# Attention and a state-space convolution on one core: absolute phases taken by ScalarE, a smaller GpSimd descriptor area, more table buffers, sines of two groups next to each other, two products joined, a new order

## The chip, the cores and the metric

The kernel runs on one core of one Trainium2 chip. The metric is the device time of one execution in microseconds (us). Three runs of the kernel before gave 783.68, 779.48 and 782.46 us, so the median is 782.46 us.

The engines are named as the profile names them: PE is the matrix engine (PEld its weight loads), DVE the vector engine, ACT the scalar engine that evaluates functions from tables, POOL the GpSimd engine, and SP the engine whose queue issues nearly all transfers. The engines run their own lists of instructions in order, and wait for each other through semaphores. SBUF is the on-chip memory, PSUM the memory into which PE writes its sums.

## The reference

Two independent parts share the core, and their results stand beside each other in the output.

```python
def _A_ref(x, wqkv, wo):                      # B=1, S=2048, D=576
    H = 32; Dh = D // H; W = 256
    qkv = (x @ wqkv).reshape(B, S, 3, H, Dh).transpose(2, 0, 3, 1, 4)
    q, k, v = qkv[0], qkv[1], qkv[2]
    scores = jnp.einsum("bhqd,bhkd->bhqk", q, k) * (Dh ** -0.5)
    mask = (idx[:, None] - idx[None, :] >= 0) & (idx[:, None] - idx[None, :] < W)
    p = _softmax(jnp.where(mask, scores, -1e9))
    return concat_heads(p @ v) @ wo
def _B_ref(u, A_re, A_im, B_re, B_im, C_re, C_im, log_dt, Dskip):   # L=2048, N=128 states
    dt = jnp.exp(log_dt)[:, None]
    P = jnp.exp((dt * (A_re + 1j * A_im))[:, :, None] * l)
    K = jnp.einsum("dn,dnl,dn->dl", C_re + 1j * C_im, P, dt * (B_re + 1j * B_im)).real
    y = irfft(rfft(pad(u)) * rfft(pad(K)))[:L] + u * Dskip
```

Part A is attention in a window of 256 over 32 heads of 18. Part B builds, for each of 576 channels, a kernel `K` of 2048 taps from 128 complex exponentials, and convolves it with the input through a Fourier transform.

## The kernel before

**Stages.** `build` runs four lists of steps, one after the other: `front`, `tables`, `first` and `rest`. In each, several generators ("streams") hold the steps of one sort of work, and the strings in `PLAN` say which stream takes its next step. A letter lets a stream go on to its next `yield`; a letter with a digit runs a piece of work that a step left behind with `post` (an eviction from PSUM, a store). The engines' lists come out in just that order, so `PLAN` sets what stands behind what on every engine. The order isn't decided by a scheduler at build time; the conditions that the generators yield are not looked at there. `SLOTS` says which of three PSUM buffers (`ring0` to `ring2`, two banks each) each step of PE takes, and two more (`pp`) belong to the projection.

**front** loads the weights and the first input, finds the scales, splits the parameters of part B into three bf16 parts that GpSimd sends through DRAM (`prep`: the `nc.gpsimd.dma_start` calls; `prepw` loads the constants `c_ca`, `c_cp`, `c_ct`, `c_cm` the same way), and starts the projection to q, k and v.

**tables** holds the rest of the projection (`P`), the first transform of the input u (`U`, `s1_u`), and the taps of part B: 18 groups q of 32 channels, each in two halves c = 2q and 2q+1 of 16 channels. For a group:

- `t_factor` (PE, L505) writes logarithms and phases of 12 factors per channel into a ring buffer; ACT takes the exponentials (`mab`, L547), and `fold` brings the phase into one turn: ACT rounds it to an integer (L511), DVE subtracts that (L514), and DVE clears the sign bit of the result into a second half of the tile (L515), so that sine and cosine can both be had from the sine function. `t_phase` does the same for 32 phases per channel (tiles `fr`, one per half). `t_mg` makes the magnitudes, which ACT raises to exponentials inside the ring buffer (L527).
- `t_sin` is one block of six ACT instructions on both halves of `fr` and on `fa` (L556, L557, L561, L562). Exponentials and sines need different function tables, so loads (`ACT_TABLE_LOAD`) stand where the list goes from one to the other.
- `t_ab` and `t_prod` are POOL's: products of the factors (L567 to L577), then two products of 1024 elements for each half (L586) into `m0` and `m1`; there is one buffer for `m1`. `t_add` on DVE (L592) adds them.
- `t_q` on DVE multiplies cosines and sines with the magnitudes in four instructions of 512 elements (L601 to L604). `t_taps` on PE (L615) sums the taps, ACT evicts them (`Kq`, L621), and `t_dft` (L631, L635) transforms them; ACT and DVE each evict half of that (L647) and SP stores it.

The end of `tables` and all of `first` also hold the first steps of attention, among them `smax1` (letters `s`), which computes scores on PE (L906 to L917) for DVE's maxima (L940). **rest** holds the rest of attention (`scores`, `pv`, `norm`, `wo`) and of the convolution (`spectra`, `inverse`, `clast`).

The pools of the tables are `tab1` with one buffer of each tile (`fa`, `t1`, `t2`, `m1`), `tab2` with two (`mab`, `tr`, `A`, `Kq`, `kst`), and `frp` with `FR` = 3.

Of the kernel before, what the change touches and what calls it, by code (L numbers as in the profile page):

```python
# [42 lines left out]
def constants():  # L43
# [23 lines left out]
    for nm, v in mult.items():  # L67
# [19 lines left out]
        "AAAVCACAAAAAVAVVV1CV1CAVAVAAVCAV1ACCVCACCVVV1VV1CVCACBBPABV1CCPV1BV1CPCPP1PVP2PP4CPAPP1PP2BPCP1P4BVP"  # L87
        "CP",
    "tables":
        "GMGPGPG5G6G1PM1GG5GP2G2PGG6P4NMMG5P1G6G5G1P2PPNM1PP4G6P1GPG2UNRP2G1MMRXPP1M1P2P4X1RMGG5NG2PRMPGP1G5X"  # L90
        "X1M1XG6X5GP2RG6PMX2RNRUPGU2PMG1UP1PG5G2M1RGNU1XXX1UG6P2MPX1G5U2RG6PX4MU1XP4RRPM1X4PXPGX5X2P1GNMUMP2P"
        "1PX1PG1RXP2M1P4PG2X1GP4PG5MUNRU1PG5G6MX4U2G6XP1U4RPRM1PPPGX5P4P2P1NMRGPP2MNXXX4G5X2G1P1P4PM1X1G6G2P4"
        "P2U4X1XMGPMGX5G5RP1PG6M1PP2X2PP4NRPP4RPMP1MG1PP2PM1UX4PP1XGRX1NP4XG2PP2GX1MG5UX4G5MPG6U2G6X4P4RU1U4R"
        "P1M1X4XX2PPXMRNU4P2GPX5P1X1MNRP2PXG1G2P4PGM1X1PG5PPXP5X4GPPP5RX5UMG5G6PG6UPPNU1UX2MRRPP4U2M1U4UU2XPP"
        "5MMRX1PGP5P6UG1U1PM1PPPG2P5UX4NRU1PMPMGM1XPP5PX1U2RU4G5P5GG5PPG6RMGXG6PP5PRX2NP6NP4PPG1MG2XPPGX5PRM1"
# [1177 lines left out]
```

## Time and profile before

| | |
|---|---|
| median of three runs | 782.46 us (779.48 to 783.68) |
| the profiled execution's own time, from first to last instruction | 784.5 us |
| busy: PE, DVE, ACT, POOL | 693.0, 588.2, 534.3, 417.3 us |
| instructions | 29499 |

The page comes from one execution. "Busy" is the time in which an engine had at least one instruction running; PE's instructions are pipelined, so its busy time holds some waiting. A row of the list of groups names the line of the kernel, the engine, the operation, the tile written and those read with their sizes, how many there are, their busy time, the mean of one in ns, and the engine's idle time ahead of them with what ended it. A row of the waits names who waited, for whom, the total, how often, and the longest.

### The profile page before, as it was taken

What the parts mean: (1) busy time and instruction counts of PE and PEld (TensorE: products, weight loads), DVE (VectorE), ACT (ScalarE), POOL (GpSimd) and SP (SyncE); (2) the same over time, 40 slices, a digit from 0 to 9 for tenths busy, and PEclk for the clock granted to TensorE, in tenths of its full rate; (3) what the DMA queues carried; (4) which work ended last, traced back from release to release, by engine and by line L of the source; (5) the groups of instructions that cost most, each with busy time, mean ns of one, the idle gap of its engine ahead of it and who ended that gap; (6) DMA issues with size and microseconds to landing.
All of it is one profiled execution on the core that took longest, in us unless ns stands there. A gap on an engine that the chain in (4) does not pass through costs nothing.

```text
span 784.5 us, 29499 instructions
## 1 busy us (share of the span) xinstructions
PE 693.0 (88%) x12956; PEld 410.8 (52%) x12956; DVE 588.2 (75%) x779; ACT 534.3 (68%) x709; POOL 417.3 (53%) x309
## 2 busy tenths in 40 slices
PE   3786878998989989997789999989989998999997
PEld 2532444565545654665544555544555554557775
DVE  5998789998998897988777888876888586852100
ACT  2369577787887777773458677775877876786622
POOL 2245867987688666866007574451553444546120
PEclk9979799999999999996999999998999999899999
DMA  8998055738247537889578777676866786555786
GB/s 309 342 215 204 7 133 149 159 83 216 51 120 182 133 70 175 230 183 277 113 238 279 247 240 231 207 243 166 245 185 203 240 256 207 170 163 159 205 258 187
DMA packets 215904, 150.67 MB, mean 192 GB/s; under 512 B 103530, under 2 KB 195818, under 8 KB 215520
## 3 DMA queue, kind: packets, MB, share of 16 engines
q1 hardware_dynamic: 214160, 146.28, 66.0%
q0 software_dynamic: 1616, 2.52, 1.1%
q8 instruction: 101, 1.65, 0.8%
q14 instruction: 27, 0.22, 0.1%
HBM read 83.50 MB, written 65.11 MB: 189 GB/s over the span
## 4 chain that ended last, share of the span: by engine, by line
PE 55%; DVE 17%; ACT 15%; issue 6%; DMA 4%; SPq 1%; POOL 0%; ACTq 0%; DVEq 0%
PE po L1020 9%; PE pp L204 9%; PE ring L204 7%; PE ring L906 5%; DVE m L940 5%; PE ring L752 4%; PE ring L982 4%; PE ring L615 4%; PE ring L718 4%; PE ring L505 2%; DMA wraw<-in_wr_dram 2%; DVE amx L192 2%; PE ring L815 2%; ACT raw L1000 2%; DVE wl L372 2%
## 5 line engine op out<-in xcount | busy, mean ns | idle before, releaser
L940 DVE TENSOR_REDUCE m<-ring 128x2 f32<-128x640 f32 (+4 forms) x256 | 190.8, 779 | 66.0 <-PE ring L914 58.2
L586 POOL TENSOR_TENSOR m<-A,tr 128x1024 f32<-128x1024 f32 x72 | 141.5, 1983 | 52.6 <-DVE m L592 43.5
L1000 ACT ACTIVATE P<-ring,esc 128x1024 f32<-128x1024 f32 (+2 forms) x86 | 90.0, 1060 | 37.1 <-PE ring L995 32.7
L1000 ACT ACTIVATE raw<-ring,esc 128x1024 f32<-128x1024 f32 (+2 forms) x74 | 77.2, 1061 | 19.4 <-PE ring L995 18.8
L734 POOL TENSOR_TENSOR t<-X 128x768 f32<-128x768 f32 x24 | 46.7, 1944 | 76.1 <-ACT X L726 75.6
L1063 POOL TENSOR_TENSOR oh<-osb,oh 128x1024 f16<-128x1024 f32 x16 | 34.1, 2133 | 59.5 <-ACT oh L1059 42.9
L914 PE MATMUL ring<-sm,idb 64*64 64x128 bf16 x896 | 56.1, 224 | 3.3 <-issue 3.1
L204 PE MATMUL pp<-xh,wh 128*128 128x512 f16 x180 | 48.1, 397 | 10.0 <-DVE qst L453 5.0
L204 PEld LDWEIGHTS <-wh 128*128 128x128 f16 x324 | 30.7, 99 | 49.1 <-issue 11.7
L615 PE MATMUL ring<-Q,m 128*32 128x64 f32 x2304 | 42.9, 231 | 12.8 <-ACT fa L511 4.1
L1055 POOL TENSOR_TENSOR osb<-osb,T 128x1024 f32<-128x1024 f32 x16 | 38.6, 2410 | 25.8 <-DVE T L1050 23.8
L592 DVE TENSOR_TENSOR m<-m,m 128x1024 f32<-128x1024 f32 x36 | 51.6, 1432 | 0.7 <-POOL m L586 0.6
L615 PEld LDWEIGHTS ring<-Q,m 128*32 128x32 f32 x2304 | 36.9, 117 | 27.2 <-ACT mab L547 5.5
L906 PEld LDWEIGHTS <-raw 54*64 54x64 f16 x704 | 28.6, 108 | 41.1 <-issue 37.7
L740 POOL TENSOR_TENSOR Y<-t,t 128x384 f32<-128x384 f32 x24 | 24.7, 1029 | 46.1 <-DVE t L734 33.8
L906 PE MATMUL ring<-K,raw 54*64 54x320 f16 (+4 forms) x576 | 44.8, 308 | 4.5 <-ACT raw L1000 0.8
L204 PE MATMUL pp<-xh,wl 128*128 128x512 f16 x180 | 48.0, 400 | 0.6 <-DVE wl L372 0.6
L567 POOL TENSOR_TENSOR tr<-tr,mab 128x768 f32<-128x768 f32 x18 | 33.3, 1850 | 28.4 <-ACT tr L562 28.4
L726 ACT ACTIVATE X<-ring 128x768 f32<-128x768 f32 x48 | 36.7, 812 | 14.3 <-PE ring L718 8.1
L995 PE MATMUL ring<-tm,idb 64*64 64x256 bf16 (+2 forms) x640 | 45.0, 257 | 0.0
L982 PEld LDWEIGHTS <-K 55*64 55x64 f16 x1280 | 28.8, 108 | 26.7 <-issue 22.7
L752 PE MATMUL ring<-Y,i 32*64 32x192 f32 x768 | 38.7, 336 | 3.3 <-issue 2.3
(171 smaller groups left out, 1725.1 us busy)
## 6 DMA issues: line engine op xcount, KB each, us to landing
gk<-kst SPq DMA_DIRECT2D x36, 256.0 KB
gx<-ust SPq DMA_DIRECT2D x16, 576.0 KB
xk<-gx SPq DMA_DIRECT2D x24, 384.0 KB
xk<-gk SPq DMA_DIRECT2D x24, 384.0 KB
h<-ho SPq DMA_DIRECT2D x48, 192.0 KB
hp<-h SPq DMA_DIRECT2D x24, 384.0 KB
K<-kz SPq DMA_DIRECT2D x14, 512.0 KB
raw<-qz SPq DMA_DIRECT2D x11, 512.0 KB
```

What stands on the lines that cost most here:

```text
L204: self.nc.tensor.matmul(ps, u, v, start=(i == 0), stop=(i == len(ops) - 1))
L586: tt(m[part], A[:, ch, a0:a0 + 8].unsqueeze(3).to_broadcast(sh), tr[:, ch, part, 0:8].unsqueeze(2).to_broadcast(sh), op=OP.mult)
L592: self.nc.vector.tensor_tensor(m[0], m[0], m[1], op=OP.add)
L615: nc.tensor.matmul(kp[32 * st:32 * st + 32, j, :], m[:, ch, 32 * term:32 * term + 32], Q[:, ch, term, :], start=(term == 0), stop=(term == ...
L734: mul(ts[i], X[:, :, :, :192].rearrange("p i s j -> p s i j"), X[:, i, :, 192:].unsqueeze(2).to_broadcast(sh), op=OP.mult)
L752: nc.tensor.matmul(ps[64 * (b % 2):64 * (b % 2) + 64, b // 2, 192 * s:192 * s + 192], self.i1[32 * b:32 * b + 32, t, o:o + 64], Y[32 * b:3 ...
L906: nc.tensor.matmul(ps[z:z + 64, b, :n], d["Q"][rr, 2 * b + pp, 64 * qb:64 * qb + 64], d["K"][rr, 2 * b + pp, k0:k1], start=True, stop=Fals ...
L914: nc.tensor.matmul(out, self.idb[rr], self.sm[rr], start=False, stop=True, skip_group_check=True)
L940: self.nc.vector.tensor_reduce(out, x, axis=AX.X, op=OP.max)
L982: nc.tensor.matmul(ps[z:z + 64, b, off:off + w], d["K"][rr, 2 * b + pp, kc:kc + 64], d["Q"][rr, 2 * b + pp, q0:q0 + w], start=(k == 0), st ...
L1000: nc.scalar.activation(P[:, :, lo:hi], ps[:, :, lo:hi], AF.Exp, scale=self.esc)
L1020: nc.tensor.matmul(po[32 * p:32 * p + 32, z, q0:q0 + w], V[64 * z:64 * z + 64, kb * 76 + 19 * p:kb * 76 + 19 * p + 32], P[p % 2][64 * z:64 ...
```

## The change

Six edits are made at once.

1. `fold` no longer clears the sign bit on DVE. `t_sin` has ACT do it, with the function `Abs`, just ahead of the sine that reads the result: two of 128x512 and one of 128x384 in each group.
2. In `t_q` the products of cosine and sine with the upper half of the magnitudes become one instruction of 1024 elements, which reads the two halves of the tile in exchanged order.
3. The descriptor area that GpSimd's transfers use in SBUF is set to 2048 bytes per partition.
4. `FR` goes from 3 to 5; `fa` gets a pool of its own with two buffers (`fap`), and `tr` one with three (`trp`).
5. All four strings of `PLAN`, and `SLOTS`, are new.
6. As part of the new order, `t_sin` of two groups stands next to each other in some places, with no load of a table between them.

```diff
 PLAN = {
     "front":
-        "AAAVCACAAAAAVAVVV1CV1CAVAVAAVCAV1ACCVCACCVVV1VV1CVCACBBPABV1CCPV1BV1CPCPP1PVP2PP4CPAPP1PP2BPCP1P4BVP"
+        "AAACVAAAVCAAAVAAV1V1VCACVVV1AAAAVCAV1VCVV1CVCCCCAPV1CVCBBCBVACAV1V1VVCPCBPPPP1CP2P4PPPP1CP2P4PBCBPP1"
...
             nc.vector.tensor_tensor(k, x, k.bitcast(I32), op=OP.subtract)
-            nc.vector.tensor_scalar(f[:, 1].bitcast(I32), k.bitcast(I32), 0x7FFFFFFF, None, op0=OP.bitwise_and)
             self.n[end] += 1
...
-            f = self.fa[q] = self.p["tab1"].tile([128, 2, GC * 12], F32, name="fa")
+            f = self.fa[q] = self.p["fap"].tile([128, 2, GC * 12], F32, name="fa")
...
         for c in (2 * q, 2 * q + 1):
             f = self.fr[c]
+            nc.scalar.activation(f[:, 1], f[:, 0], AF.Abs)
             nc.scalar.activation(f[:, 0], f[:, 0], AF.Sin, scale=-TWO_PI)
             nc.scalar.activation(f[:, 1], f[:, 1], AF.Sin, scale=-TWO_PI, bias=self.halfpi)
         f = self.fa.pop(q)
-        tr = self.tr[q] = self.p["tab2"].tile([128, GC, 2, 12], F32, name="tr")
+        tr = self.tr[q] = self.p["trp"].tile([128, GC, 2, 12], F32, name="tr")
         v = lambda z: z.rearrange("p (c m) -> p c m", m=12)
+        nc.scalar.activation(f[:, 1], f[:, 0], AF.Abs)
...
-        tt(Q[:, :, 0, 32:64], cs, m[:, :, 32:64], op=OP.mult)
+        tt(Q[:, :, :, 32:64], f.rearrange("p i (c m) -> p c i m", m=32)[:, :, ::-1],
+           m[:, :, 32:64].unsqueeze(2).to_broadcast([128, HC, 2, 32]), op=OP.mult)
         tt(Q[:, :, 0, 0:32], cs[:, :, ::-1], m[:, :, 0:32], op=OP.mult)
-        tt(Q[:, :, 1, 32:64], sn, m[:, :, 32:64], op=OP.mult)
...
-            self.FR = 3
-            for n, b in (("tab1", 1), ("tab2", 2), ("frp", self.FR), ("P0", 2), ("Qp", 2)):
+            self.FR = 5
+            for n, b in (("tab1", 1), ("tab2", 2), ("frp", self.FR), ("P0", 2), ("Qp", 2), ("fap", 2), ("trp", 3)):
...
-    nc = _bacc.Bacc("TRN2", target_bir_lowering=False, num_devices=1)
+    nc = _bacc.Bacc("TRN2", target_bir_lowering=False, num_devices=1, dynamic_dma_scratch_size=2048)
```

How the new order stands on the engines is seen at two places. The first is ACT's list, where it takes the sines of a group. Before, each group's block has a load ahead of it and one behind it (buffer numbers are left out; `tr` holds the sines of the factors, `halfpi` is the constant that makes a cosine):

```order
L450 ACTIVATE qst<-pp 128x512
L556 ACT_TABLE_LOAD
L556 ACTIVATE fr<-fr 128x512
L557 ACTIVATE fr<-fr,halfpi 128x512
L556 ACTIVATE fr<-fr 128x512
L557 ACTIVATE fr<-fr,halfpi 128x512
L561 ACTIVATE tr<-fa 128x32x12
L562 ACTIVATE tr<-fa,halfpi 128x32x12
L511 ACTIVATE fr<-ring 128x512
L547 ACT_TABLE_LOAD
```

In the changed kernel, at one such place, the sines of a group are followed by three evictions and the two shown first here, and then by the sines of the next group, with the rows of L556 and L562 as the new `Abs`; the load for the exponentials comes only behind them:

```order
L623 ACTIVATE Kq_1281<-ring_1248 128x256
L623 ACTIVATE Kq_1281<-ring_1284 128x256
L556 ACTIVATE fr_1156<-fr_1156 128x512
L557 ACTIVATE fr_1156<-fr_1156 128x512
L558 ACTIVATE fr_1156<-fr_1156,halfpi_153 128x512
L556 ACTIVATE fr_1194<-fr_1194 128x512
L557 ACTIVATE fr_1194<-fr_1194 128x512
L558 ACTIVATE fr_1194<-fr_1194,halfpi_153 128x512
L562 ACTIVATE fa_1154<-fa_1154 128x384
L563 ACTIVATE tr_1364<-fa_1154 128x32x12
L564 ACTIVATE tr_1364<-fa_1154,halfpi_153 128x32x12
L547 ACT_TABLE_LOAD
```

The block of a group is nine rows instead of six. Over the whole list there were 37 loads of a table and there are 27: 18 groups had 18 loads ahead of their sines and have 13, so five pairs of groups share one, and the loads that go back to the exponentials (at L527 and L547) fall from 18 to 13; one stands at the start in both.

The second place is DVE's list near the start of `tables`, with the folds (`fr`, `fa`), the low halves of q and k (`qst`), and the products `Q`. Before:

```order
L514 TENSOR_TENSOR fr_516<-ring_485,fr_516 128x512
L515 TENSOR_SCALAR fr_516<-fr_516 128x512
L514 TENSOR_TENSOR fa_520<-ring_470,fa_520 128x384
L515 TENSOR_SCALAR fa_520<-fa_520 128x384
L453 SCALAR_TENSOR_TENSOR qst_556<-pp_450,qst_556 128x512
L601 TENSOR_TENSOR Q_588<-fr_474,ring_507 128x16x32
L602 TENSOR_TENSOR Q_588<-fr_474,ring_507 128x16x32
L603 TENSOR_TENSOR Q_588<-fr_474,ring_507 128x16x32
L604 SCALAR_TENSOR_TENSOR Q_588<-fr_474,ring_507 128x16x32
L592 TENSOR_TENSOR m0_579<-m0_579,m1_580 128x1024
```

And now, where L515 is the subtraction and L594 the sum of POOL's products:

```order
L515 TENSOR_TENSOR fr_593<-ring_571,fr_593 128x512
L515 TENSOR_TENSOR fr_595<-ring_591,fr_595 128x512
L515 TENSOR_TENSOR fa_634<-ring_562,fa_634 128x384
L515 TENSOR_TENSOR fa_639<-ring_617,fa_639 128x384
L454 SCALAR_TENSOR_TENSOR qst_621<-pp_499,qst_621 128x512
L594 TENSOR_TENSOR m0_602<-m0_602,m1_603 128x1024
L454 SCALAR_TENSOR_TENSOR qst_678<-pp_573,qst_678 128x512
L603 TENSOR_TENSOR Q_698<-fr_518,ring_680 128x32x32
L605 TENSOR_TENSOR Q_698<-fr_518,ring_680 128x16x32
L606 SCALAR_TENSOR_TENSOR Q_698<-fr_518,ring_680 128x16x32
```

The 54 rows that cleared sign bits are gone, four rows of products have become three, and the folds of the factors of two groups (`fa_634`, `fa_639`) follow each other, which one buffer for `fa` didn't allow. In the tables POOL's list has the same rows in the same order as before, and the same 12 transfers ahead of them; SP issues the same number of transfers. PE has the same matmuls: up to the last taps its list holds the same ones but for 16 more at L906, 12 more at L914, 4 more at L917, 12 fewer at L982 and 4 fewer at L995.

More of the change, by code (lines that the diff above doesn't have):

```diff
@@ L86 @@
     "front":
[L87 to L88 removed]
+        "AAACVAAAVCAAAVAAV1V1VCACVVV1AAAAVCAV1VCVV1CVCCCCAPV1CVCBBCBVACAV1V1VVCPCBPPPP1CP2P4PPPP1CP2P4PBCBPP1"
+        "PP",
     "tables":
[L90 to L91 removed]
@@ new lines @@
+        "PMNRU4X1P4GP2NXX2PG1PPP1G2X5P2RRMM1UUU2U1PGG5XPX1MMPM1GG6RXX1MG5P4P4G6PP1P1P2NGG1G2P2P4P4XX5PX2MGG5G"
+        "G5G6G6PPU4M1UUPPRRRMUNNX4RXX1X4X4U1PU2U4P1P1XP2UU1U2U4PUX1P2UNU2RU1PPPPP1P2P4XGX2G1X4PP5PRX5P4P4MM1P"
+        "G2PP5GGX4X4RMPG5PPP5PG6G5G6MM1XX1MMM1RPGNPPPP5G1G2PMMP5M1XX1PRPRPPXX2NRP5RMPGG5PPPP5G6X5X4PXXPX1X1GG"
+        "5G6XPP5PPPNRNP1P2MM1PPX4PX5X2X4X4GGPRRMP1P2G1G5XG6X1GRG2MG5M1G6PP1MU4GP4NG1G2GG5G6PPMP2M1MMM1XP4PPX1"
+        "UUMNU1PUU2XX5RRP1X2PP2XX1P1P4UP4RU4U2U1U4GP2G5NG6NPURPPP1MP2PPM1P4UU2U1PXU4RRX1P1MMPPM1XMX5PRX2MM1XP"
@@ new lines @@
+        "2GG1PPX4X1MNG2GP1PG5P2P4GG6G5P6P6GG1PPRG2P1GG6RPG5G6RMP5M1XX1XX4P4P2X2PPPPPNXMPGX5G5RRP6XG6P6X4P5PPP"
+        "5X1X1NRNXPX4X2P5PP4ZPPP5UGGG5G6G1PPPP5RRMG2M1MX4X4PPX5PPPUUU2PPU1UU1U2P5XU4P6RMX1M1MMM1MPP5PPP1PXX4X"
+        "4GPG5G6GX1NRG1G2XX2X5PP1P2P6MP2GGG5ZZG6RPM1PMRPG5G6U4XPNPRUP4P1UU1U2P4P2PP1P4UUPP4U2X1U1ZP2UMM1MMM1X"
+        "X1MNNPPPPRXRXP1X2P2X1X5GPRRGPG1G2X4X4G5G6P4MM1P6MPXX1X4PP6P1P1XX2X5P2NMP2M1GGG1G2PPPPG5G6MUUPRNRU4U2"
+        "U1UU4U1P4X4GP1U2P4P2U4G5G6PGP1MG5G6PM1ZXX1PPP5P2RRMMXM1MPPPX1PPss2sss2s2ss2sss2s2PP5P4sss2X4Ps2sss2s"
@@ new lines @@
+        "s4vassa1vs2s2ss2LaLsvvva1saa1s2s2Lss2vvv1ss2sas2c3c2aa1Lvssls6a1ass2s2c6n3aa1a1vss2aksa1aa1s2vkkscs2"
+        "c1asc3c6s4a1vvsss2s2ds2Lc2sd1s2ava1kcc1naasc3vd4s2va1a1saa1s2vsc2s2sads2a1ssld1kvsn1s2c6c3s2kkcLLLs2"
+        "c1ss6aa1sdss2n6sv1n4d4Lvvd4d1s2s2sss2s2ass2vala1saa1la1vvss2ss2s2vkss2ass2n3vc6s4aa1a1c2sdn1d1d4fs2c"
+        "3ss2aa1n6ssvs2Laa1svvv1s2Ls2sLss6s2ss2ss2cc1ss2aaa1a1svs2saa1aa1s2fee1asvnva1ss2as2ss2vaa1a1ssvvs2s2"
+        "d4Lss4an3s2n4n1ss2vnaa1a1aa1kn6asa1fs2kvfvvv1aa1see1s2asc2a1vLLs2asn3s6a1dd1c6c3ncc1aa1llLLsss2s2van"
@@ new lines @@
+        "4a1sn1ss2s2vss2sks2vss2n4aa1svsvls2s2skks2ss2dc2c6c3d1s4ss2cc1llaa1d4ss2dlsvs2Lss2d1d4aa1sLLvaa1e4s2"
+        "saa1s6c6ss2n3vvaa1ss2sss2s2aan6v1c2a1vsva1sas2s2asa1a1kvvn1kss2ks2n6aa1svvs2ss2sss2ss2vcc1c3s2fvs4ss"
+        "dlLLs2d1ys2c2c6c3scc1s2sLs6aaa1da1c2afa1Lsvd4d4d1n4nn3s2vv1c6ee1asLva1ss2aa1s2ss2vsn1sn6ke4s2s2ava1s"
+        "as2ss2n4sa1ss2s2asa1ss2s2vlaaskvs2va1a1ss4c3as2a1ss2aa1kncLc1vaa1sdd1s2ss6aa1LLssn3s2s2n1kkvssss2s2s"
+        "2vvayasv1vvn6s2ss2a1a1aa1sn4vssls2s2ssvs2d4s2s2ava1ac2aa1ss4Lva1ss2as2a1ss2vasLc6Lava1a1s2sas6ca1c1L"
@@ new lines @@
+        "sc3aa1vnn3ks2ass2a1dvd1d4d4c2v1ss2saa1svs2Ls2sas2a1ss2vn1lssss2s2s2avaa1sss2vs2vs4a1aa1fssvfan6s2ss2"
+        "s2Laa1La1Lnvee1sc6cvfc1s2ss6sc3s2aa1svvv1fs2c2e4sc6s2c3faa1s4fesksve1s2ss2s2svas2ss2vaa1a1ss2ss2aa1s"
+        "vss2s2ass2vaa1sss2s2vss2a1aa1kckc1kaLLLa1ss6n3nvaaa1a1lc2ddd1Lsss2vn4n1ve4s2ksd1n6ss2s2ss2vv1sc6cc1l"
+        "ls2svs2asss2s2vsa1aa1c3c2ee1svs2c6sc3kks2s2scc1s2vaa1ss2ss2kvvlasc6lls4wa1ww1s2ss6aa1aa1ddd4d4d1n4d1"
+        "cd4n4vvc2c1aaa1a1wc3wn3n1kc2kdnw1n3vvd1n1aaa1a1wkaa1akffc6c3n6v1wwww4a1w4w1Lcw1c1e4e4c6van6a1aaa1vfc"
@@ L143 @@
+    "2120102102102102101201021012012012021020120210210210201021021102102102102012101210210212012012012012"
+    "0210210120120120120120120121021020102102110210201201201202101201201210210120120120120121201201201201"
+    "201202012012012012120121021"
 )
```

63 lines of the change are left out of this document (19 added, 44 removed).

## The prediction

> **What bounds the kernel now.** I read the page for the shares of the engines, then split the span at 62 us (first load for sines) and at 384 us (last rows of `t_dft`).
>
> ```profile
> 62.00:384.00 322.00, 282.87 (x4027) 168.58 (x4025) 280.35 (x388) 239.20 (x381) 233.90 (x183) 0.95 0.60 145
> 384.00:784.50 400.50, 371.00 (x8797) 221.01 (x8789) 256.70 (x335) 269.16 (x295) 166.09 (x104) 0.98 0.71 215
> PE 55%; DVE 17%; ACT 15%; issue 6%; DMA 4%; SPq 1%; POOL 0%; ACTq 0%; DVEq 0%
> ```
>
> The columns of the windows are the stretch, its length, and the busy time of PE, PEld, DVE, ACT and POOL, then PE's granted clock, the share of the transfer engines and GB/s. Up to the last taps PE is busy 282.9 of 322 us and DVE 280.4; PE idles 39.1 us. Behind it PE is busy 371.0 of 400.5 us and no other engine is near that. In the chain (third row) PE has 55%, DVE 17%, ACT 15%. So the second stretch is PE's, and what the edits to the tables can win lies in the first one: PE's 39.1 us of idle time, and no more. Its waits there, by releaser:
>
> ```profile
> PE pp L204 <- DVE qst L453: 5.3, 5, 2.2
> PE ring L615 <- ACT fa L511: 4.1, 1, 4.1
> PE ring L615 <- DVE fa L514: 2.5, 3, 1.4
> PE ring L505 <- ACT ust L498: 2.3, 4, 1.0
> ...
> PE ring L631 <- ACT ust L498: 0.2, 1, 0.2
> ```
>
> These are the first four and the last of 30 rows. The 16 that name DVE sum to 22.1 us, the 13 that name ACT to 15.6, one transfer has 0.4. None is long: PE is held up a little everywhere, because an eviction or a factor comes late from an engine whose list is nearly full. POOL is held by DVE too, since its second product needs the one buffer of `m1` back:
>
> ```profile
> POOL m L586 <- DVE m L592: 43.5, 17, 5.1
> POOL tr L567 <- ACT tr L562: 28.4, 14, 7.9
> ```
>
> **DVE gives up 54 us.**
>
> ```profile
> L592 DVE TENSOR_TENSOR m<-m,m 128x1024 f32<-128x1024 f32 x36 | 51.6, 1432 | 0.7 <-POOL m L586 0.6
> L515 DVE TENSOR_SCALAR fr<-fr 128x512 int32<-128x512 int32 x36 | 35.7, 992 | 1.2
> L514 DVE TENSOR_TENSOR fr<-ring,fr 128x512 f32<-128x512 f32 x36 | 24.6, 682 | 5.2 <-ACT fr L511 4.9
> L601 DVE TENSOR_TENSOR Q<-fr,ring 128x512 f32<-128x512 f32 x36 | 24.5, 680 | 7.6 <-ACT ring L527 4.9 <-PE ring L615 2.0 <-ACT fr L557 0.7
> L603 DVE TENSOR_TENSOR Q<-fr,ring 128x512 f32<-128x512 f32 x36 | 24.4, 679 | 0.0
> L515 DVE TENSOR_SCALAR fa<-fa 128x384 int32<-128x384 int32 x18 | 13.2, 733 | 0.6
> L514 DVE TENSOR_TENSOR fa<-ring,fa 128x384 f32<-128x384 f32 x18 | 9.9, 551 | 8.1 <-ACT fa L511 8.0
> 60.24 0.43 DVE L515 TENSOR_SCALAR fr<-fr 128x512 int32<-128x512 int32 x1
> 61.77 0.36 DVE L515 TENSOR_SCALAR fa<-fa 128x384 int32<-128x384 int32 x1
> ```
>
> Both groups of L515 go: 35.7 + 13.2 = 48.9 us, of which 48.1 lie in the stretch (the last two rows run ahead of it, 0.43 and 0.36 us). The joined product of 1024 elements isn't in the trace. It can't be shorter than one of its halves (0.68), and the longest mean for 1024 elements is L592's 1.432 against 2 x 0.68 = 1.36 for the pair, so the 36 of them save between 24.4 us and nothing, or cost 2.6. L514's two sizes give 0.682 - 0.551 = 0.131 us for 128 elements, so 1.21 us for 1024; I take that: 36 x 0.15 = 5.4 us saved. DVE's list falls from 280.4 to 280.4 - 48.1 - 5.4 = 226.9 us.
>
> **ACT takes on 19 us.**
>
> ```profile
> L556 ACT ACT_TABLE_LOAD x18 | 23.1, 1283 | 0.3
> L556 ACT ACTIVATE fr<-fr 128x512 f32<-128x512 f32 x36 | 22.4, 623 | 0.4 <-DVE fr L515 0.2
> L511 ACT ACTIVATE fr<-ring 128x512 int32<-128x512 f32 x36 | 21.5, 598 | 11.9 <-PE ring L505 9.4 <-POOL wi L338 1.7 <-DVE Q L604 0.6
> L547 ACT ACT_TABLE_LOAD x14 | 18.0, 1283 | 5.1 <-PE ring L505 4.9
> L561 ACT ACTIVATE tr<-fa 128x384 f32<-128x384 f32 x18 | 9.1, 507 | 0.0
> 67.00 0.60 ACT L511 ACTIVATE fr<-ring 128x512 int32<-128x512 f32 x1
> 67.61 1.28 ACT L547 ACT_TABLE_LOAD   x1
> 68.91 0.49 ACT L547 ACTIVATE mab<-ring 128x384 f32<-128x384 f32 x1
> ```
>
> An `Abs` has no row; a sine without a bias tile of the same sizes has 0.623 and 0.507 us, a copy 0.598. By the sines 36 x 0.623 + 18 x 0.507 = 31.5 us come on (by the copy 1 us less). Ten loads of 1.283 us go, 12.8 us. Net +18.7: ACT's list in the stretch grows from 239.2 to 257.9 us of 322. The last three rows show what a change of tables costs: the instruction ahead ends at 67.60, the load runs from 67.61 to 68.89, the next starts at 68.91, so hardly anything beside the 1.28 us.
>
> The Trainium skill, ScalarE: Activation LUTs, section "What ACT_TABLE_LOAD costs", adds a drain of 1.38 us to each load, 2.66 us together; by that ten loads would give back 26.6 us and ACT would grow by only 4.9. The trace shows no such drain between these three rows.
>
> **The rest of the edits.** The small descriptor area touches GpSimd's 12 transfers at the start.
>
> ```profile
> q0 software_dynamic: 1616, 2.52, 1.1%
> 37.16 0.56 POOL L252 DMA_DIRECT2D c_ca<-in_c_ca_dram  x1
> 40.28 0.51 POOL L308 DMA_DIRECT2D Tim<-splim  x1 [0.43 <-issue]
> Tre<-splre POOLq DMA_DIRECT2D x1, 432.0 KB, 6.4
> Tim<-splim POOLq DMA_DIRECT2D x1, 432.0 KB, 7.0
> c_cm<-in_c_cm_dram POOLq DMA_DIRECT2D x1, 384.0 KB, 5.0
> 56.43 0.33 PE L505 MATMUL ring<-c_ca,Tre 96*128 96x384 bf16 x1
> ```
>
> Six of them are issued within 3.1 us and the last one lands at 40.3 + 0.5 + 7.0 = 47.8 us; PE reads it first at 56.4. If nothing has to wait for room, the cost is nothing. At worst each waits until the one ahead has landed: 4 x 5.0 + 6.4 us put the last issue at 63.6 and its landing near 70.6 us, 14 us after PE asks for it. I take nothing, since the whole queue moves only 1616 packets in the span, and keep the 14 us for the range. The added buffers cost no instruction; what they hide is in the sum below. The new order of `first` and `rest` rearranges the same work in a stretch where PE idles 400.5 - 371.0 = 29.5 us. I take zero and keep 4 us either way, a seventh of that idle time, which is a choice and not a measurement.
>
> **The sum.** It can be made in two ways. At most all 22.1 us that PE waits for DVE go, with nothing in return. Or the four engines stay as well filled together as before: 282.9 + 280.4 + 239.2 + 233.9 = 1036.4 us in 322 us is a sum of shares of 3.22; with 282.9 + 226.9 + 257.9 + 233.9 = 1001.6 us the stretch would last 311.2 us, 10.8 less. The first leaves out that ACT, which takes over from DVE as the fullest helper (257.9 against 226.9 us), will release PE later at places. The second leaves out that POOL, behind DVE for 43.5 us, will get `m1` back sooner, and that five `fr`, two `fa` and three `tr` let PE and ACT run further ahead. I take 15 us between the two. What is late next is PE itself, 282.9 us of then 307, with ACT behind it. The front isn't shortened. So the profiled execution would last 784.5 - 15 = 769.5 us; the median of the runs is 2.0 us below that execution's own time (782.46 against 784.5), which gives **767.5 us**.
>
> **Rivals.** *ACT takes it back.* The `Abs` stands between the fold and the sine in ACT's list, where DVE did it beside ACT, so a group's block there lasts nine instructions, 1.75 us longer, and evictions from `ring` and `pp` stand behind it. PE already waits 15.6 us for ACT; if those waits double, as the waits for DVE shrink by about as much, nothing is left: 780 to 784 us. Against it, ACT idles 82.8 us in the stretch and mostly because PE has nothing for it:
>
> ```profile
> ACT Kq L621 <- PE ring L615: 29.8, 18, 9.8
> ACT kst L647 <- PE ring L635: 10.4, 8, 2.9
> ```
>
> *Slower, by the same place.* If PE stands at ACT's blocks in nearly every group, with its three `ring` buffers full, the whole 18.7 us lengthens the stretch while DVE's relief opens nothing: 782.5 + 18.7 = 801 us, or 792 with half of it. It decides from the point at which each of the 18 groups loses over 1 us more to ACT than it gains from DVE (22.1 / 18 = 1.2 us at most). For it speaks the one wait of 4.1 us for `fa` from ACT; against it that the other 12 rows of ACT reach 2.3 us at most in total each.
>
> The Trainium skill, ScalarE: Activation LUTs, section "Rules for kernel authors", speaks for this rival: simple operations belong on VectorE, which it calls up to about three times faster per element, in bf16. In this trace, in fp32, the 128x512 took 0.992 us on DVE and the sine of that size 0.623 on ACT, so the trace does not agree.
>
> *The small area stalls GpSimd*: the tables start up to 14 us late, and with the gain the time is about 781. It is the case in which the change doesn't do what it says, as the room for more buffers isn't free. *More than forecast*: if the free time on DVE and the added buffers let PE be filled to 96% in the stretch, more than the 93% behind it (371.0 of 400.5), it lasts 282.9 / 0.96 = 295 us, 27 less: 755 us. For it speaks that no wait of PE there is longer than 4.1 us; against it that PE has never been that full over such a length.
>
> **How the numbers follow.** A measurement of this kernel can tell about 0.5%, 4 us, from no change: below 778.5 is faster, above 786.4 slower. The forecast, with a gain of 8 to 23 us, has 0.60; more than that 0.11; ACT or the small area taking it back 0.18; slower 0.11. Forecast alone: 759 to 775. The range reaches up to the rivals without a gain and down to the one with more: 753 to 783. Faster 0.71, same 0.18, slower 0.11.
>
> **What would show it.** DVE's busy time should fall from 588 to about 534 us, with no row that clears sign bits and a joined product near 1.2 us; ACT's should rise from 534 to about 553, with 27 loads of 1.28 us. The last taps should end near 367 us instead of 382, PE's waits for DVE ahead of that should halve and its waits for ACT grow by some 5 us; POOL's 43.5 us for the sum on DVE should shrink. Behind the last taps the span should still be about 400 us. The prediction is wrong if the last taps come no earlier (then it is ACT, and PE's waits name it), if PE's first L505 comes later than 56 us (then it is the area), or if the second stretch differs by over 4 us.

## The result and the profile after

The changed kernel takes 788.91 us (median of 20 runs, 782.15 to 795.07) where the kernel before, measured beside it, takes 782.48: a ratio of 1.0081, with an interval of 1.0054 to 1.0108. It is slower by some 6 us, where 15 us less were forecast. The profiled execution took 794.09 us with a span of 792.3, so it is one of the slower ones, 5 us above the median.

The page of the changed kernel, with the engines' busy time and the chain that ended last:

```profile
PE 693.5 (88%) x12956; PEld 405.8 (51%) x12956; DVE 544.7 (69%) x689; ACT 547.8 (69%) x753; POOL 413.9 (52%) x309
PE 46%; DVE 17%; ACT 15%; DMA 11%; issue 6%; SPq 4%; POOL 2%; ACTq 0%; DVEq 0%; POOLq 0%
```

DVE has 43 us less than before (588.2) and ACT 13.5 more (534.3). In the chain 11% are transfers now (4% before) and 4% SP's queue (1%). The windows, cut at the first load for sines and at the last rows of `t_dft` (columns as in the prediction), first the kernel before in its tables, then the changed one in all three stretches:

```profile
61.30:384.00 322.70, 283.55 (x4028) 168.83 (x4027) 281.02 (x389) 239.90 (x381) 233.90 (x183) 0.95 0.60 145
```

```profile
0.00:69.70 69.70, 40.43 (x145) 22.16 (x146) 48.87 (x55) 25.20 (x35) 16.24 (x22) 0.89 0.91 276
69.70:391.50 321.80, 288.67 (x4068) 167.06 (x4067) 244.93 (x307) 252.83 (x424) 232.15 (x183) 0.94 0.57 138
391.50:792.30 400.80, 364.41 (x8753) 216.58 (x8745) 250.92 (x329) 269.76 (x296) 165.50 (x104) 0.99 0.71 217
```

Two things are to be seen. The tables start 8.4 us later (69.7 instead of 61.3). And from there to the last rows of `t_dft` 321.8 us pass where 322.7 passed before, although DVE is busy 36 us less in them. Behind them 400.8 us pass against 400.5, but the 400.5 of this one execution of the kernel before is not typical of its order, as the experiments show.

The groups of the edited instructions came out, row by row, as they were costed: the joined product (L603), the two sizes of `Abs` (L556, L562), and 27 loads of a table:

```profile
L603 DVE TENSOR_TENSOR Q<-fr,ring 128x1024 f32<-128x1024 f32 x36 | 43.7, 1214 | 6.9 <-ACT ring L527 6.5 <-PE ring L617 0.2
L556 ACT ACTIVATE fr<-fr 128x512 f32<-128x512 f32 x36 | 22.4, 623 | 1.9 <-DVE fr L515 1.9
L562 ACT ACTIVATE fa<-fa 128x384 f32<-128x384 f32 x18 | 9.1, 507 | 0.0
L557 ACT ACT_TABLE_LOAD x13 | 16.7, 1283 | 0.2
L527 ACT ACT_TABLE_LOAD x7 | 9.0, 1283 | 3.5 <-PE ring L506 3.1 <-DVE m L942 0.4
L547 ACT ACT_TABLE_LOAD x6 | 7.7, 1283 | 7.1 <-PE ring L506 7.1
L292 ACT ACT_TABLE_LOAD x1 | 1.3, 1283 | 0.7 <-PEq L1265 0.7
```

What PE waits for in the middle stretch (the first four rows of that view; all of them add up to 24.3 us for DVE, 7.5 for ACT):

```profile
PE pp L205 <- DVE xh L386: 4.0, 2, 2.5
PE ring L617 <- DVE m L594: 3.7, 2, 2.3
PE ring L506 <- DVE fa L515: 3.4, 4, 1.5
PE ring L506 <- DVE Q L606: 3.3, 2, 2.6
```

Its waits for DVE did not halve: 22.8 us before over the same stretch, 24.3 now, with an eighth less work on DVE. Its waits for ACT did not grow by 5 us but fell from 15.6 to 7.5, and POOL's wait for the sum on DVE did not shrink: 43.5 us before, 55.7 now.

The late start is read from the chain of the changed kernel between 52 and 67 us, and from the rows of SP's queue (start, duration, engine, line, transfer):

```profile
56.84 0.61 DVE qst L454
...
57.83 2.43 SPq L467
60.26 0.05 issue
60.31 6.26 DMA qz<-qst
```

```profile
49.16 0.58 SPq L413 DMA_DIRECT2D qz<-ones  x1
49.79 0.57 SPq L413 DMA_DIRECT2D kz<-ones  x1
60.31 2.59 SPq L468 DMA_DIRECT2D qz<-qst  x1
66.80 0.60 ACT L451 ACTIVATE qst<-pp 128x512 f16<-128x512 f32 x1 [5.49 <-DMA qz<-qst]
```

The new order of `front` puts the two transfers of 1280 KB that fill `qz` and `kz` with ones ahead of the stores of `qst`. Some stores behind them take 2.4 to 2.6 us to be issued, the next `qst` has no buffer until one of them has landed, and ACT stands for 5.49 us. Before, the two came behind ten of these stores:

```profile
54.39 0.36 SPq L467 DMA_DIRECT2D qz<-qst  x1
54.85 0.32 SPq L412 DMA_DIRECT2D qz<-ones  x1
55.21 0.46 SPq L412 DMA_DIRECT2D kz<-ones  x1
```

### The profile page after: what moved, and what is told of

Its sections match the earlier page's. It is cut to its first block, busy times and chain, and to the rows that moved or that the text cites. A ratio compares the mean times of both kernels' runs of the same rounds, so it can differ in the third digit from the quotient of the medians.

```text
span 792.3 us, 29461 instructions
## 1 busy us (share of the span) xinstructions
PE 693.5 (88%) x12956; PEld 405.8 (51%) x12956; DVE 544.7 (69%) x689; ACT 547.8 (69%) x753; POOL 413.9 (52%) x309
## 4 chain that ended last, share of the span: by engine, by line
PE 46%; DVE 17%; ACT 15%; DMA 11%; issue 6%; SPq 4%; POOL 2%; ACTq 0%; DVEq 0%; POOLq 0%
PE pp L205 9%; PE po L1022 6%; PE ring L908 4%; DVE m L942 4%; PE ring L984 4%; PE ring L205 3%; PE ring L617 3%; PE ring L720 3%; DVE m L594 3%; PE ring L754 3%; DMA K<-kz 3%; PE ring L506 2%; DMA wraw<-in_wr_dram 2%; PE ring L633 2%; DVE amx L193 2%
## 5 line engine op out<-in xcount | busy, mean ns | idle before, releaser
L942 DVE TENSOR_REDUCE m<-ring 128x2 f32<-128x640 f32 (+4 forms) x256 | 189.1, 778 | 48.9 <-PE ring L916 40.9
L588 POOL TENSOR_TENSOR m<-A,tr 128x1024 f32<-128x1024 f32 x72 | 144.1, 2018 | 60.5 <-DVE m L594 55.7
L1002 ACT ACTIVATE raw<-ring,esc 128x1024 f32<-128x1024 f32 (+2 forms) x74 | 77.0, 1060 | 22.8 <-PE ring L997 22.4
L205 PE MATMUL pp<-xh,wh 128*128 128x512 f16 x180 | 49.9, 409 | 12.3 <-ACT vst L406 6.7
L594 DVE TENSOR_TENSOR m<-m,m 128x1024 f32<-128x1024 f32 x36 | 54.4, 1511 | 2.0 <-POOL m L588 1.8
L908 PE MATMUL ring<-K,raw 54*64 54x320 f16 (+4 forms) x576 | 43.5, 311 | 13.3 <-DMA K<-kz 4.6
L916 PE MATMUL ring<-sm,idb 64*64 64x128 bf16 x896 | 52.7, 217 | 0.4 <-issue 0.4
L205 PE MATMUL pp<-xh,wl 128*128 128x512 f16 x180 | 50.1, 413 | 1.5 <-DVE wl L373 1.5
L908 PEld LDWEIGHTS <-raw 54*64 54x64 f16 x704 | 26.8, 106 | 44.7 <-issue 41.5
L742 POOL TENSOR_TENSOR Y<-t,t 128x384 f32<-128x384 f32 x24 | 24.0, 1001 | 48.9 <-DVE t L736 29.2
L603 DVE TENSOR_TENSOR Q<-fr,ring 128x1024 f32<-128x1024 f32 x36 | 43.7, 1214 | 6.9 <-ACT ring L527 6.5
## 6 DMA issues: line engine op xcount, KB each, us to landing
xk<-gx SPq DMA_DIRECT2D x24, 384.0 KB
xk<-gk SPq DMA_DIRECT2D x24, 384.0 KB
hp<-h SPq DMA_DIRECT2D x24, 384.0 KB
```

The source lines that it names most:

```text
L205: self.nc.tensor.matmul(ps, u, v, start=(i == 0), stop=(i == len(ops) - 1))
L588: tt(m[part], A[:, ch, a0:a0 + 8].unsqueeze(3).to_broadcast(sh), tr[:, ch, part, 0:8].unsqueeze(2).to_broadcast(sh), op=OP.mult)
L594: self.nc.vector.tensor_tensor(m[0], m[0], m[1], op=OP.add)
L908: nc.tensor.matmul(ps[z:z + 64, b, :n], d["Q"][rr, 2 * b + pp, 64 * qb:64 * qb + 64], d["K"][rr, 2 * b + pp, k0:k1], start=True, stop=Fals ...
L916: nc.tensor.matmul(out, self.idb[rr], self.sm[rr], start=False, stop=True, skip_group_check=True)
L942: self.nc.vector.tensor_reduce(out, x, axis=AX.X, op=OP.max)
```

## The experiments

Twelve kernels were run, each with a profile and five rounds of timing against the kernel before on the same chip. "Tables" are the time from the first load for sines to the start of the last row of `t_dft` in the profiled execution. Single executions of one kernel differ by some 5 us either way (the kernel before: 774 to 785 us in the runs beside the first four), so the ratios decide and the tables' times only place a difference. In the eleven profiles with the front of before, the first load comes at 59.8 to 62.6 us.

| kernel | ratio to the kernel before (interval) | first load for sines, us | tables, us |
|---|---|---|---|
| before | 1 | 61.3 | 322.7 |
| changed | 1.0081 (1.0054 to 1.0108) | 69.7 | 321.4 |
| e1 changed, ones last | 1.0056 (1.0020 to 1.0092) | 65.0 | 320.9 |
| e2 changed, front of before | 1.0009 (0.9978 to 1.0040) | 61.9 | 315.0 |
| e3 changed, whole order of before | 1.0317 (1.0271 to 1.0363) | 62.3 | 345.9 |
| e4 the same, old buffers and area | 1.0326 (1.0273 to 1.0378) | 61.6 | 353.0 |
| e5 before, product joined | 1.0007 (0.9973 to 1.0041) | 61.7 | 324.5 |
| e6 before, `Abs` on ACT | 1.0326 (1.0281 to 1.0372) | 61.7 | 347.0 |
| e7 e2 with signs cleared on DVE | 1.0373 (1.0316 to 1.0430) | 60.4 | 346.9 |
| e8 e2 with no signs cleared | 0.9906 (0.9865 to 0.9947) | 59.8 | 310.5 |
| e9 before, no signs cleared | 1.0013 (0.9983 to 1.0043) | 60.8 | 323.7 |
| e10 before, both clear signs | 1.0342 (1.0297 to 1.0388) | 62.2 | 348.0 |
| e11 e1, weights earlier | 1.0047 (1.0012 to 1.0081) | 67.1 | 319.3 |
| e12 e2 with ten loads back | 1.0244 (1.0198 to 1.0290) | 62.6 | 334.4 |

### Which part of the change costs: e1 to e4

The order of the front was taken back in part (e1) and whole (e2):

```diff
 e1, end of "front":
-... V1 V1 V V C P C B P P P P1 C P2 P4 P P P P1 C P2 P4 P B C B P P1 P P
+... V1 V1 V C P C B P P P P1 C P2 P4 P P P P1 C P2 P4 P B C B P P1 V P P
 e2: the whole string "front" of the kernel before
```

> The changed kernel with one step moved: the two transfers that fill the rows of q and k with -32768 (1280 KB each, L413) are issued at the end of the front, behind the first stores of q, as in the kernel before, and not ahead of them. Theory 1 (the queue): these 2.6 MB delay the first stores of q, all three qst buffers stay taken, and ACT waits 5.5 us for one; here that wait is gone, the first load for sines comes near 63 us instead of 69.7, and the time falls by about 6 us to a ratio of 1.000 against before (0.996 to 1.003). Rival (the front's order of work on DVE and ACT): the first load stays near 68 us and the ratio near 1.008. Rival (PE-bound anyway): the load comes early, but the last taps still end near 388 us.

> The changed kernel with the whole order of the front as it was before; tables, first and rest in the new order. Theory 1: as the run with the two transfers moved, first load for sines at 61 to 63 us, ratio 0.996 to 1.002. Rival (the front's other moves cost too): clearly below that run, by 2 us and more. Rival (the small descriptor area is what delays the start): the first load stays past 66 us, since the area is small here as well.

With the front of before the ratio falls from 1.0081 to 1.0009: the new front costs about 0.7%, some 6 us, and all the rest of the change together comes to nothing. The two transfers of ones are 4.7 of the 8.4 us of late start in single profiles, and perhaps a third of the 6 us by the ratio (1.0056, whose interval overlaps both others, so the share itself isn't shown). The first load of e1 lies between what its Theory 1 and its rival expected.

Then the strings of `PLAN` and `SLOTS` were taken back whole, with all other edits kept (e3), and with the old pools (of `fa` and `tr` too) and the old area (e4):

```diff
 e3: PLAN and SLOTS of the kernel before
 e4: the same, and
-            self.FR = 5
+            self.FR = 3
-    ... ("Qp", 2), ("fap", 2), ("trp", 3)):
+    ... ("Qp", 2)):
-    ... num_devices=1, dynamic_dma_scratch_size=2048)
+    ... num_devices=1)
```

> Edits 1 to 4 (Abs on ACT, joined product, small area, more buffers) with all four strings of the order and the slots of before. ACT's list grows by 31 us here, as all 37 table loads stay, DVE's shrinks by 54. Theory 2 (the edits are worth what the prediction said, and it is the new order that loses it): 8 to 15 us faster than before, ratio 0.981 to 0.990. Rival (ACT takes back what DVE gives): 0.998 to 1.012, with PE's waits for ACT in the tables well above the 15.6 us of before.

> Edits 1 and 2 alone (Abs on ACT, joined product) in the old order, with the old pools and the old descriptor area. In the old order nothing runs further ahead than the old buffers allow, so theory 2 expects the same as with the new pools and the small area, within 0.3%. If the area or the added buffers matter by themselves, the two runs differ by more than that.

In the old order the edits make the kernel 3.2% slower, 25 us, all of it in the tables; both theories of e3 had it lower. Buffers and area move nothing that can be measured there (1.0317 against 1.0326); in the new order they were not taken back. So the edits themselves cost 25 us in the old order, and the new order with the front of before brings about as much back.

It does so in the tables alone. From e3 to e2 they are 30.9 us shorter, and the stretch behind them is 6.5 us longer (391.7 and 398.2 us). The other profiles agree: behind the tables, six of the old order (e3 to e6, e9, e10) take 391.7 to 394.3 us and the seven of the new order 396.3 to 403.0, though 38 matmuls fewer are left for it there. Only the profile of the kernel before, with its 400.5 us, stands apart from its own order. The windows of e6 and then of e2, and a row of PE's waits in e2 between 62 and 408 us:

```profile
408.70:802.00 393.30, 368.55 (x8797) 220.99 (x8789) 256.20 (x335) 268.70 (x295) 166.16 (x104) 0.98 0.72 219
376.90:775.10 398.20, 364.49 (x8759) 216.95 (x8755) 251.02 (x329) 269.95 (x296) 165.60 (x104) 0.99 0.72 219
PE ring L907 <- DMA K<-kz: 4.8, 1, 4.8
```

PE stands 3.8 to 7.3 us for the transfers that load `K` in every profile of the new order, and never in one of the old. That this wait is what makes the stretch longer is a reading of the traces; no run takes back `first` and `rest` alone.

### Which edit: e5 to e8

The two edits to the arithmetic were made one at a time in the kernel before, e5 joining the product and e6 taking the `Abs` to ACT (each as in the diff of the change). Then, in e2, the signs were cleared by DVE again (e7), and by nobody (e8, where the cosines of `fa` are changed as those of `fr` shown here):

```diff
 e7, in fold, and no Abs in t_sin:
+            nc.vector.tensor_scalar(f[:, 1].bitcast(I32), k.bitcast(I32), 0x7FFFFFFF, None, op0=OP.bitwise_and)
 e8, in t_sin:
-            nc.scalar.activation(f[:, 1], f[:, 0], AF.Abs)
-            nc.scalar.activation(f[:, 0], f[:, 0], AF.Sin, scale=-TWO_PI)
-            nc.scalar.activation(f[:, 1], f[:, 1], AF.Sin, scale=-TWO_PI, bias=self.halfpi)
+            nc.scalar.activation(f[:, 1], f[:, 0], AF.Sin, scale=-TWO_PI, bias=self.halfpi)
+            nc.scalar.activation(f[:, 0], f[:, 0], AF.Sin, scale=-TWO_PI)
```

> The kernel before with one edit alone: the two products that read the upper half of the magnitudes are joined (order, pools, sign clearing as before). It takes about 5 us off VectorE in the tables stage (36 products of 1.21 us in the place of 72). Theory A (the tables stage goes with ScalarE's row, VectorE's time is not on the path): ratio 1.000 within 0.003. Theory B (the prediction's own: the stage goes with the summed busy time of its engines): about 2 us less, 0.997. Theory C (the hand-written order fits only the durations it was made for, and any departure costs): slower, 1.003 to 1.010.

> The kernel before with the other edit alone: the absolute phases go from VectorE to ScalarE (order and pools as before, products not joined). With both edits in the old order the ratio was 1.0326. Theory A: ScalarE's 36 x 0.62 + 18 x 0.51 = 31.5 us come into the tables stage nearly in full and VectorE's 48 us less buy nothing, so the ratio is 1.030 to 1.040, the same as with both edits within 0.005. Theory B: VectorE gives up more than ScalarE takes, so at most 1.00. Theory C: anything from 1.01 up, and with the joined product alone the rest of the 1.0326.

> The changed kernel with the order of the front of before (that version gave 1.0009), and the signs cleared on VectorE again, in the same step as the fold; the new order of tables and what follows, the new buffers, the 27 table loads and the joined product stay. ScalarE loses 31.5 us, VectorE gets 48 us back. Theory A: the 10 loads fewer (12.8 us of ScalarE) come out as time, so 0.975 to 0.990 and faster than before and than the change. Theory B: VectorE's row is again 281 us in the stage, the sum of the engines is about that of before, so 0.995 to 1.01. Theory C: the order was made for the shorter VectorE and longer ScalarE, so slower than 1.0009, 1.01 to 1.04.

> [...] ScalarE loses 31.5 us against the version with 1.0009, VectorE nothing. Theory A (ScalarE's row sets the tables stage in the new order too): 20 to 30 us less, 0.963 to 0.975. Theory B (sum of the engines): about a quarter of 31.5 us, 8 us, 0.99. Theory C or a stage that TensorE and its waits on VectorE bound: within 0.005 of 1.000.

The joined product is worth nothing by itself (1.0007), and the `Abs` on ACT carries the whole 3.3% of the old order. The tables of e6, with 26.7 us more on ACT than before and 43 less on DVE, are 24.3 us longer:

```profile
61.70:408.70 347.00, 291.12 (x4025) 171.28 (x4023) 238.01 (x335) 266.62 (x434) 226.53 (x183) 0.93 0.55 136
```

Here Theory A holds, but e7 goes against it: with the signs back on DVE the kernel should have become faster than before, and it is 28 us slower than e2. PE's waits in the tables of e7 name DVE in the first rows:

```profile
60.40:407.30 346.90, 294.90 (x4061) 169.44 (x4059) 292.44 (x361) 227.47 (x371) 235.06 (x183) 0.92 0.55 134
61.90:376.90 315.00, 285.28 (x4059) 165.98 (x4056) 244.33 (x306) 252.29 (x424) 233.18 (x183) 0.95 0.60 147
```

```profile
PE ring L615 <- DVE m L592: 9.8, 6, 2.8
PE ring L505 <- DVE Q L604: 8.6, 6, 2.4
PE pp L204 <- DVE xh L385: 8.0, 2, 4.2
PE ring L615 <- DVE Q L604: 5.7, 4, 2.7
```

The first fence holds the windows of e7 and, below it, of e2. All rows of that view together: PE waits 48.4 us for DVE in e7 and 22.4 in e2, and all its waits grow by 22.4 us. The other 9.6 us of the 31.9 that the tables are longer are PE's own busy time, for the same matmuls at a lower granted clock (0.92 against 0.95). So the new order has no room for 48 us more on DVE, as the old one had none for 31 us more on ACT. Which of the two, the order or the `Abs`, is said to cost or to win depends on which is changed first: in the old order the `Abs` costs 25 us, in the new one it wins 28.

e8 shows the reverse: 31 us fewer on ACT bring about 8 us (0.9906 against 1.0009). That is the size that Theory B names, but its sum of the engines fails in e7 and e9. e8 is the one version that is faster than both kernels; it leaves the absolute values out, so that its cosines are sines of arguments up to 3/2 pi.

### What the relief of DVE is worth: e9 and e10

The prediction's main term was put to the test by itself: no signs cleared in the kernel before, in its own order (e9, the edit of e8 without the `Abs` row, and L515 left out), and signs cleared twice, by DVE as before and by ACT as in the change (e10, whose `Abs` of `fa` isn't shown here):

```diff
 e9, in fold:
-            nc.vector.tensor_scalar(f[:, 1].bitcast(I32), k.bitcast(I32), 0x7FFFFFFF, None, op0=OP.bitwise_and)
 e10, in t_sin:
+            nc.scalar.activation(f[:, 1], f[:, 0], AF.Abs)
```

> The kernel before in all but one thing: no signs are cleared at all, the cosines are taken from the phases with their sign (that leaves the absolute values out of the computation). VectorE loses its 48 us in the tables stage, ScalarE gets nothing. This is the prediction's main term by itself, without the price on ScalarE. The prediction's rate (10.8 to 22.1 us for 54 us off VectorE) gives 10 to 20 us less here, 0.974 to 0.988. Theory D, drawn from the runs with the absolute phases on either engine in either order (work added to an engine comes out at 0.65 to 0.9 us per us, work taken off returns little, as the no-sign version of the new order did: 8 us for 31): 3 to 10 us less, 0.987 to 0.996. Theory A (VectorE's time is not on the path at all in the old order): 1.000 within 0.004.

> The kernel before with ScalarE's absolute phases added while VectorE clears the signs as before (the work is done twice). ScalarE gets 31.5 us, VectorE loses nothing. With VectorE relieved the ratio was 1.0326, so this run less that one is what the relief is worth once ScalarE is loaded. Theory A: the same 1.033 within 0.005. Theory D: 1.035 to 1.045. The prediction's rates (relief of 10 to 20 us, so an addition of 35 to 45 us behind the 1.0326): 1.045 to 1.058.

DVE's 49 us are worth nothing that can be measured in the old order: 1.0013 with nothing put in their place, and with ACT loaded the relief makes 1.0342 into 1.0326, within the intervals. Theory A holds in both. The tables of e9 are as long as before with 38 us less on DVE:

```profile
60.80:384.70 323.90, 283.04 (x4030) 167.26 (x4031) 242.99 (x335) 242.92 (x381) 228.75 (x183) 0.95 0.59 145
```

Where the time went is seen in DVE's own waits, of the kernel before and then of e9 (engine, what waits, for whom: total, times, longest):

```profile
DVE ust L498 <- PE ring L493: 8.4, 7, 2.3
DVE fa L514 <- ACT fa L511: 8.0, 6, 2.8
DVE qst L453 <- ACT qst L450: 5.2, 7, 1.7
DVE fr L514 <- ACT fr L511: 4.9, 5, 1.3
```

```profile
DVE fa L514 <- ACT fa L511: 15.0, 7, 3.7
DVE fr L514 <- ACT fr L511: 13.8, 18, 1.8
DVE ust L498 <- PE ring L493: 13.7, 9, 2.7
DVE qst L453 <- ACT qst L450: 9.5, 8, 1.8
```

The folds waited 12.9 us for ACT's rounding and wait 28.8 now. All rows of the view together go from 38.7 to 80.0 us: DVE is busy 38 us less and waits 41 us more, 27 of them for ACT and 13 for PE. And PE's waits for DVE hardly moved (22.8 to 19.8 us over the same stretch). That fits rows of DVE that stand behind ACT's and not behind DVE's own work; the totals show it, the single waits were not followed.

### The rest of the front, and the loads: e11 and e12

In e1 the chain of work that ended last runs for 5.3 us (50.06 to 55.34) through an eviction and conversions of weights on ACT and DVE. The expectation of e11 below reads this as a wait of PE, but PE had work for most of it and stood for only 1.4 us ahead of 55.34. e11 lets these conversions (`C`) run earlier, ahead of projection steps:

```diff
-... V1 V1 V C P C B P P P P1 C P2 P4 P P P P1 C P2 P4 P B C B P P1 V P P
+... V1 V1 V C C P C B P P P P1 C P2 P4 P P P P1 P2 P4 P B C B P P1 V P P
```

> The changed kernel with three steps of its front moved: the two transfers of ones behind the last stores (that alone gave 1.0056 and a first table load for the sines at 65.02 us), and two conversions of weights put one and several projection steps earlier, ahead of the evictions that ScalarE and VectorE did first in that run while TensorE waited for weights from 50.06 to 55.34 us. If these are the rest of what the front costs, the first load comes at 60.5 to 62.5 us and the ratio falls to that of the version with the whole front of before, 1.001 within 0.003. If the rest of the loss lies elsewhere in the front (the transpositions' splits, GpSimd), the load stays at 64 to 66 us and the ratio at 1.004 to 1.007.

The first load comes at 67.10 us, later than in e1, PE stands 3.0 us at the same place, and the ratio is that of e1 within the intervals. Moved in this way, the conversions bring nothing back. What the rest of the front's cost is remains open.

e12 puts the ten loads back into e2 with one exponential of a single column ahead of each group's sines:

```diff
+        nc.scalar.activation(self.toggle, self.halfpi, AF.Exp)
         for c in (2 * q, 2 * q + 1):
```

> The version with the new order, the front of before and both edits (1.0009), with the ten saved table loads put back: one exponential of a single column is issued ahead of each group's sines, so that the sines of two groups no longer share a load (27 loads become 37, 10 x 1.283 us and 18 tiny instructions, some 15 us of ScalarE in the tables stage; nothing else is moved). Theory D (work added to an engine in a fixed order comes out at 0.65 to 0.9 us per us): 9 to 14 us more, 1.012 to 1.019, and the tables stage 324 to 329 us long where that version's took 315. If ScalarE's row pays in the new order only at the rate that the no-sign version showed (8 us for 31): 4 us, 1.004 to 1.008. If the loads lie wholly beside other work: 1.001 within 0.003.

```profile
L558 ACT ACT_TABLE_LOAD x18 | 23.1, 1283 | 0.3
L554 ACT ACT_TABLE_LOAD x5 | 6.4, 1283 | 0.1
L554 ACT ACTIVATE toggle<-halfpi 128x1 f32<-128x1 f32 x18 | 3.6, 203 | 0.1
62.60:397.20 334.60, 292.47 (x4062) 169.38 (x4061) 244.71 (x306) 267.31 (x450) 230.73 (x183) 0.93 0.58 138
```

ACT gets 12.8 + 3.6 = 16.4 us of rows (15.0 of busy time in the tables), and the time grows from 1.0009 to 1.0244 of the kernel before, 18 us (14 to 23 by the two intervals): more than Theory D's upper end. The shared loads are worth about as much as they take. By the Trainium skill, ScalarE: Activation LUTs, section "What ACT_TABLE_LOAD costs", a load with its drain takes 2.66 us, so ten would be worth 26.6 us, and 30 with the tiny rows; the run lies under that and near the rows' own 1.283 us.

## Why the prediction was wrong

**The rows were right.** The joined product was put at 1.21 us and has 1.214; the `Abs` at 31.5 us and has 22.4 + 9.1; the loads went from 37 to 27. DVE's groups lost 48.9 us of cleared signs and 5.2 by the joined product, as worked out; its busy time fell by 43.5 only, partly because other rows grew (`xh` by 3.6, the sum L594 by 2.8, `xl` by 2.4 us). The 48.9 us were no fixed length either: the rows of 128x512 had taken from 0.43 to 2.25 us each. ACT rose by 13.5 instead of 18.7 us, because its rows overlap, so that they add less busy time than their sum. The second row here starts 0.41 us behind the first, which lasts 0.51:

```profile
73.90 0.51 ACT L562 ACTIVATE fa<-fa 128x384 f32<-128x384 f32 x1
74.31 0.51 ACT L563 ACTIVATE tr<-fa 128x384 f32<-128x384 f32 x1
```

In e6 the 31.5 us of `Abs` rows are 26.7 us of busy time. The small area and the buffers cost nothing in the old order, as assumed (e3 against e4).

**The sum failed.** "I take 15 us between the two": both ends, 10.8 us from the summed shares and 22.1 us from PE's waits for DVE, give DVE's time a value, and e9 measures that of the 48.9 us, in the order of before, as nothing: +1.0 us (from 1.3 us less to 3.4 more). The end of 22.1 us took the engine that a wait names for the one that sets it. But DVE itself waited in this stretch, 23.7 us for ACT and 14.0 for PE: its folds for ACT's rounding, its low halves of `qst` for ACT's high halves. The end of 10.8 us took the four engines for vessels that share one sum; in lists with a fixed order they do not share. The sign of it was there before the run: DVE idled 322.7 - 281.0 = 41.7 us in the stretch, and its waits for ACT and PE fill nearly all of it.

**ACT was priced too low.** The forecast let ACT's 18.7 us pass inside the same sum. The rival "Slower, by the same place" had the mechanism, that ACT's longer blocks lengthen the stretch "while DVE's relief opens nothing", and e10 shows it by itself: 31.5 us of rows on ACT, 26.8 us of busy time in the tables, cost 27 us of time (1.0342). It was given a chance of 0.11 because PE's own waits for ACT were short. They are short in e6 too, 5.5 us at most in one row; all of PE's waits in the tables grow there by 16.2 us, 11.4 of them for ACT and 4.9 for DVE, and its own busy time by 7.6 us at a lower clock.

**What the change won back.** The new order, with ten loads fewer and the front of before, turns the 25 us that the edits cost (e4) into nothing (e2). By e12 the ten loads are up to 18 of these 25 us. The forecast counted the loads only as ACT's busy time, 12.8 us against 31.5, and gave the order no value of its own beyond the free time.

**The stretch behind the tables.** "I take zero and keep 4 us either way" holds only against the one profile of the kernel before. Against the six other profiles of the old order the new one takes 6 us longer on the mean there (399.5 against 393.1), which eats up most of what the tables of e2 win (315.0 against 322.7 to 324.5 in the kernel before, e5 and e9).

**The front.** "The front isn't shortened" left out that it could be lengthened. It was, by 8.4 us in the profile and 0.7% in the ratio; this is what makes the changed kernel slower than before, since without it the ratio is 1.0009 (e2). Part of it is the two large transfers ahead of the stores on SP's queue, a move that stands in SP's order and was not priced: 4.7 us of the late start, and perhaps a third of the 0.7%. The rest is unexplained.

**The signs that were set.** "The prediction is wrong if the last taps come no earlier (then it is ACT, and PE's waits name it)". The last taps ended 5.7 us later (388.2 us against 382.5), and the last row of `t_dft` came 7.1 us later (391.1 against 384.0). It is ACT in the edits, but PE's waits in the changed kernel do not name it: they name DVE, which e9 shows to be waiting itself. The second sign came too: PE's first L505 (L506 now) stands at 62.7 us instead of 56.4. But it isn't the area, as the prediction has it: with the small area and the front of before it stands at 56.8 (e3) and 57.5 (e2). It is the new front.

The Trainium skill, ScalarE: Activation LUTs, section "Rules for kernel authors", would have simple operations (it names relu, max, min, add and mul) on VectorE. For the absolute value, in the old order, that holds by 25 us (e6); in the new one the reverse holds by 28 us (e7 against e2). Neither follows from the mean length of the row (0.992 us on DVE, 0.623 on ACT). What fits both is that each order was laid out for its own split of the work; no run tests that by itself.

## What to carry to other kernels

Before a wait is credited to the engine that it names, look at what that engine waits for: if its idle time goes to a third engine, taking work off it only makes it wait longer, and one run with the work left out altogether prices that at once. In the two hand-written orders here, work added to an engine cost from over half of its length to all of it, and work taken away from the kernel that an order was made for returned little or nothing, so an edit and its new order are to be measured apart. One profile of the kernel before is one execution: where the parts of a span are compared, other runs of the same order show what is usual. A new order also moves transfers in the queues: price each large one that comes to stand ahead of stores whose buffers are waited for.

## What the runs showed that was not expected

Nearly a third of the time that was added in the tables was no wait. In e6 against before and in e7 against e2, PE's busy time there grew by 7.6 and 9.6 us for practically the same matmuls, at a mean granted clock of 0.93 and 0.92 instead of 0.95. How this can come about is seen in two neighbouring windows of the changed kernel:

```profile
80.00:90.00 10.00, 5.54 (x69) 2.63 (x73) 8.26 (x10) 9.92 (x16) 8.84 (x6) 1.00 0.08 16
90.00:100.00 10.00, 7.96 (x112) 4.25 (x102) 6.44 (x9) 8.56 (x16) 9.76 (x9) 0.57 0.41 108
```

PE is busy 5.5 of 10 us in the first, and the clock granted in the next is 0.57. The Trainium skill, TensorE: Matmul & The Clock Gate, section "Part 1: The HAM clock gate (the "warmup" mystery)", says that the clock is set by how busy the array has been lately and falls to half after an idle window. These windows agree with the first part: the lower clock follows the less busy window, though PE's longest idle time in the two is 2.65 us. If that is the way, a late helper is paid for twice; no run tests it by itself.

Several of the transfers behind the two fills with ones take 1.7 to 2.6 us to be issued, where most take 0.3 to 0.4. In the kernel before, the loads of three constants stood there in the place of the stores that ACT waits for now. Why the issues are slow there isn't shown. The first two loads:

```profile
55.72 2.17 SPq L1198 DMA_DIRECT2D wk<-in_c_wk_dram  x1
57.93 2.40 SPq L1200 DMA_DIRECT2D dsk<-in_dsk_dram  x1
```
